# Theta's projection and dense product in scaled fp16 parts, maxima spread through the product banks, and a new order

## Chip, cores and metric

One Trainium2 chip, one of its cores. The metric is the device time of one execution in microseconds, here the median of several. The inputs are drawn anew by a fixed rule and are float32 and float64 on the host's side; the output is float32.

## What is computed

The reference is bucketed attention followed by a mixing block, cut here to its formulas (B=4 batches, H=8 heads, S=768 positions, D=64, model width 512):

```python
mask = q_bucket[:, :, :, None] == k_bucket[:, :, None, :]      # 6 sign bits of q @ proj, k @ proj
scores = np.where(mask, scale * np.matmul(q, k.transpose(0, 1, 3, 2)), -1000000000.0)
attn = np.exp(scores - np.max(scores, axis=-1, keepdims=True))
attn = attn / (np.sum(attn, axis=-1, keepdims=True) + 1e-09)
x = np.matmul(attn, v)                                         # then laid out as B, S, H * D
theta = x @ w_theta
zr, zi = x * np.cos(theta), x * np.sin(theta)
u = x + np.einsum('ts,bsd->btd', w_tok_r, zr) + np.einsum('ts,bsd->btd', w_tok_i, zi)
return (u + np.maximum(u @ w_ch, 0.0)).astype(np.float32)
```

## The kernel before, in words

The work is a list of small operations, each for one engine. A table of numbers, `ORDER`, gives the order in which they are issued; every engine works through its own share of it in that order, and an instruction that waits holds back all that stand behind it on its engine. Entries `f0` to `f3` of the table are fillers: one product of constants (`idle_`) of 512 columns into one of the product banks, whose result nobody reads. Nothing is planned at run time.

Attention runs in 96 steps: batch (4) by head pair (4) by query tile (6), two heads to a step. For each head TensorE makes 128 x 768 scores into a pair of PSUM banks (`scores`, operation `dst` for one head in batch 0, `st` for both heads after it), VectorE takes the row maximum, ScalarE the exponential (`pf`) and its fp16 part (`pp`, L704), GpSimd the remainder (L711), a DMA turns both parts, and TensorE sums them with `v` in 18 short products (`pv`). Batch 0 uses float32 scores plus a product of bit codes; batches 1 to 3 use split operands (`hl`) and a mask.

The mixing block of a batch (`moe`) follows its 24 steps and is woven between the steps of the next batch. Per batch there are six token tiles, and for each: four transposes of x (`transposed`, L815), the upper part by ScalarE (L820) and the remainder by VectorE (L824), then twelve products with `w_theta` in three terms, hi·hi, hi·lo and lo·hi (`project`, recorded at L96 as `wth,h_x` and `wth,l_x`), phase and sine (L856, L859, L881), `f`, `z` (L893 to L904), then 36 products of token mixing (`z,wtk`, fp16), `u` (L933), again transposes and parts, twelve products with `w_ch` (`wch,h_u`, `wch,l_u`), the sum with the positive part (`fin`, L945, VectorE) and the store. `h_x`, `l_x`, `wth`, `h_u`, `l_u` and `wch` are float32 words in the rounded format F32R.

PSUM has eight banks: three pairs for scores (`s`) and the rest for products (`m`, four homes). A scale for `v` (16 times) and for the token weights (6 times) needs a maximum over all partitions. `spread_max` makes it: a transpose to one row, a maximum of that row by VectorE, and a product with ones that puts it on every partition. Row and column stand in spare halves of score banks, listed by hand in `SPREAD`. `pow2_scale` then turns the maximum into a power of two and its inverse with three small VectorE operations on 128 partitions.

```python
            terms = [(a, bb, c) for c in range(NC) for a, bb in (("hi", 0), ("hi", 1), ("lo", 0))]
...
                        mm(res["ps"][:, : cols.stop - cols.start], u[a][:, c], w[bb][:, c, cols], n == 0, n == len(terms) - 1)
```

## Time and profile before

| | before |
|---|---|
| median of 3 runs | 734.14 us (729.14 to 736.46) |
| the profiled execution | 729.0 us, of it 727.2 us span |
| TensorE busy | 714.3 us (98%) |
| VectorE / ScalarE / GpSimd busy | 588.3 / 535.4 / 430.3 us |
| granted TensorE clock | 1.00 over the span |

The span runs from the first to the last instruction; 1.8 us of the execution lie around it. Busy times are unions of an engine's instructions. A product's recorded duration contains the time in which the next one already streams, so what a product costs is read from one start to the next, not from its duration.

### The profile page before, as it was taken

How to read it: one execution, taken by the hardware profiler on the slowest of the kernel's cores; microseconds unless marked ns; L12 is line 12 of the kernel's file. 1: busy time of each engine (PE TensorE's matmuls, PEld its weight loads, DVE VectorE, ACT ScalarE, POOL GpSimd, SP SyncE). 2: the span in 40 equal slices, each digit the busy share in tenths (PEclk: the TensorE clock that was granted, in tenths of full speed). 3: DMA queues.
4: the chain of work that ended last, by engine and by line, in shares of the span. 5: the costliest groups of instructions: out<-in, count | busy, mean ns of one | idle time of the engine just before them, and what ended most of it. 6: DMA issues, size and time to landing. Idle time of an engine off the chain costs nothing.

```text
span 727.2 us, 17462 instructions
## 1 busy us (share of the span) xinstructions
PE 714.3 (98%) x6644; PEld 468.2 (64%) x6644; DVE 588.3 (81%) x1343; ACT 535.4 (74%) x718; POOL 430.3 (59%) x461
## 2 busy tenths in 40 slices
PE   8999999999999999999999999999999999999998
PEld 3455555566756566787856676777656676884456
DVE  5879986889999999989888886989997887747223
ACT  3786887979999778778998775778986776756000
POOL 4576576776557776976666767556666666611000
PEclk9999999999999999999999999999999999999999
DMA  8899999997786999999867998997769989940002
GB/s 338 178 213 224 198 184 215 177 239 169 172 180 143 195 216 190 231 195 209 167 113 150 205 169 170 184 209 119 135 125 169 168 169 170 167 95 16 1 0 87
DMA packets 324044, 120.97 MB, mean 166 GB/s; under 512 B 306316, under 2 KB 313848, under 8 KB 323960
## 3 DMA queue, kind: packets, MB, share of 16 engines
q1 hardware_dynamic: 323960, 119.86, 82.1%
q8 instruction: 52, 0.85, 0.5%
q14 instruction: 32, 0.26, 0.1%
HBM read 32.56 MB, written 6.29 MB: 53 GB/s over the span
## 4 chain that ended last, share of the span: by engine, by line
PE 69%; DVE 11%; DMA 8%; ACT 7%; issue 3%; POOL 1%; SPq 0%; DVEq 0%; ACTq 0%; POOLq 0%
PE ps L96 67%; DMA pt<-pp 6%; DVE pf L678 3%; PE ps L815 2%; ACT pp L704 2%; ACT pf L695 2%; DVE mk L674 1%; POOL pp L711 1%; DVE l_x L824 1%; DMA raw<-in_wt_dram 1%; ACT pf L698 1%; DVE f L893 1%; DVE raw L331 1%; DVE vv L404 1%; ACT n L856 1%
## 5 line engine op out<-in xcount | busy, mean ns | idle before, releaser
L711 POOL TENSOR_TENSOR pp<-pf,pp 128x384 f16<-128x384 f32 x372 | 347.1, 957 | 186.5 <-ACT pp L704 141.5
L96 PE MATMUL ps<-z,wtk 128*128 128x512 f16 x864 | 203.2, 379 | 0.4 <-DVE rows L536 0.4
L695 ACT ACTIVATE pf<-pf,mc 128x768 f32<-128x768 f32 x144 | 133.3, 930 | 53.5 <-DVE mc L681 41.5
L704 ACT ACTIVATE pp<-pf 128x768 f16<-128x768 f32 x192 | 159.7, 838 | 15.4 <-DMA pt<-pp 12.9
L678 DVE CUSTOM_DVE_ANT_1 pf<-ps,mk 128x768 f32<-128x768 f32 x144 | 136.6, 952 | 31.7 <-POOL pp L711 15.1
L96 PEld LDWEIGHTS <-pt 128*128 128x128 f16 x3456 | 120.4, 97 | 27.7 <-issue 6.9
L96 PEld LDWEIGHTS <-wtk 128*128 128x128 f16 x864 | 78.6, 98 | 87.4 <-issue 4.0
L96 PE MATMUL ps<-vv,pt 128*128 128x65 f16 (+1 forms) x3456 | 129.5, 193 | 1.0 <-DVE x L933 0.4
L96 PE MATMUL ps<-hl 64*128 64x512 f32 (+1 forms) x864 | 97.7, 352 | 1.3 <-DVE mc L678 1.3
L96 PEld LDWEIGHTS ps<-hl 64*128 64x128 f32 x864 | 73.2, 184 | 27.8 <-issue 9.4
L674 DVE TENSOR_SCALAR mk<-kb,qc 128x768 bf16<-128x768 bf16 x144 | 85.1, 604 | 0.3
L96 PE MATMUL ps<-nat 64*128 64x512 f32 (+1 forms) x192 | 71.0, 506 | 0.3 <-ACT pf L698 0.2
L96 PE MATMUL ps<-wth,h_x 128*128 128x512 f32 x192 | 65.2, 420 | 0.2 <-DVE l_x L824 0.2
L96 PE MATMUL ps<-wch,h_u 128*128 128x512 f32 (+1 forms) x200 | 64.4, 405 | 0.0
L698 ACT ACTIVATE pf<-ps,mc 128x768 f32<-128x768 f32 x48 | 46.9, 985 | 22.5 <-DVE mc L691 16.0
L96 PE MATMUL ps<-idle 128*128 128x512 f16 x196 | 59.6, 391 | 3.4 <-DVE l_x L824 1.2
L904 POOL TENSOR_TENSOR z<-f,z 128x512 f16<-128x512 f32 x25 | 32.3, 1295 | 47.1 <-ACT z L898 34.7
L685 DVE TENSOR_REDUCE mc<-ps 128x1 f32<-128x768 f32 x48 | 45.1, 948 | 11.6 <-PE ps L96 10.5
L820 ACT ACTIVATE h_u<-ps 128x512 fp32r<-128x512 f32 x24 | 14.2, 591 | 50.0 <-PE ps L815 33.8
L96 PEld LDWEIGHTS ps<-nat 64*128 64x128 f32 x192 | 28.8, 186 | 25.9 <-issue 17.9
L893 DVE SCALAR_TENSOR_TENSOR f<-x,zsc,z 128x512 f32<-128x512 f32 x48 | 37.4, 798 | 4.4 <-ACT z L882 2.7
L96 PEld LDWEIGHTS ps<-wch,h_u 128*128 128x128 f32 x200 | 35.7, 188 | 7.8 <-ACT rows L543 0.3
(125 smaller groups left out, 961.5 us busy)
## 6 DMA issues: line engine op xcount, KB each, us to landing
nat<-in_qk_dram SPq DMA_DIRECT2D x32, 384.0 KB, 3.9
raw<-in_wt_dram SPq DMA_DIRECT2D x12, 768.0 KB, 5.1
vb<-in_v_dram SPq DMA_DIRECT2D x16, 384.0 KB, 4.2
out_dram<-x SPq DMA_DIRECT2D x23, 256.0 KB, 2.8
kb<-rows SPq DMA_DIRECT2D x48, 96.0 KB, 2.6
pt<-pp SPq DMA_TRANSPOSE x192, 4.2
w_th<-in_moe_w_theta_dram SPq DMA_DIRECT2D x4, 512.0 KB, 5.5
w_ch<-in_moe_w_ch_dram SPq DMA_DIRECT2D x8, 256.0 KB, 4.0
```

The costliest lines, as they stand in the source:

```text
L96: PE.matmul(out_, l, r, start=start, stop=stop, skip_group_check=True)
L674: DVE.tensor_scalar(u["mk"][:, :, : S // 3], t["code"][:, j].rearrange("p (a n) -> p a n", a=3), t["qc"][:, i, j : j + 1], -APART, ALU.not ...
L678: DVE.tensor_tensor_reduce(u["pf"].rearrange("p (a n) -> p a n", a=3), st[j].rearrange("p (a n) -> p a n", a=3), u["mk"][:, :, : S // 3], ...
L685: DVE.tensor_reduce(col(0), st[j], AX.X, ALU.max, negate=True)
L695: ACT.activation(u["pf"], u["pf"], AF.Exp, bias=col(2), scale=1.0 / math.sqrt(D))
L698: ACT.activation(u["pf"], st[j], AF.Exp, bias=col(2), scale=col(1))
L704: ACT.activation(u["pp"][:, 0], u["pf"], AF.Copy)
L711: return lambda: eng.tensor_tensor(u["pp"][:, 1, cols], u["pf"][:, cols], u["pp"][:, 0, cols], ALU.subtract)
L815: PE.transpose(u["pt"][:, c], src()[:, c * P : (c + 1) * P], ident)
L820: ACT.activation(u["hi"], u["pt"], AF.Copy)
L893: DVE.scalar_tensor_tensor(u["f"], tl[b][:, tt], zsc[:, b : b + 1], t["zw"][r][:, tt], ALU.mult, ALU.mult)
L904: return lambda: eng.tensor_tensor(t["z"][r, 1][:, tt], u["f"], t["z"][r, 0][:, tt], ALU.subtract)
```

## The change

What it does, by parts:

- `wth`, `wch` and the turned parts of x and u become fp16. So that they fit fp16's range, each operand is scaled by powers of two: `w_theta` and `w_ch` by a maximum over all their values (new `prep_theta` and `prep_ch`, in place of `split_weight`), x by the largest scale of its batch, u per row. The scales enter as column operands of operations that were there (`xh`, `xl`, `turns`, `rest`, the sines), which now multiply and subtract instead of only subtracting.
- The dense product's end becomes two operations: `relu` (scale and positive part, ScalarE or VectorE) into a temporary tile, and `fin` (the sum, VectorE or GpSimd).
- `spread_max` takes two short holds of product banks instead of the hand-listed spare halves, and forms the power of two on the one-partition value before it is spread; the maxima become 24 instead of 22.
- Step 0 loads k before q, makes its sign products in another order, and splits both heads' scores into a first part (`dsa`) that doesn't wait for the signs and a second (`dsb`).
- `ORDER` and the numbers behind it are new throughout. It holds 289 fillers instead of 196. The tile counts of `pp` and the slots of the raw weights change with it.

The diff, cut to its core (the table of the order is left out; the rows below show what it does):

```diff
-    wth = [wp.tile([P, NC, DM], F32R, name=f"wth{i}") for i in range(2)]
+    wth = [wp.tile([P, NC, DM], F16, name=f"wth{i}") for i in range(2)]
...
-    def pow2_scale(amax, inv, s):
-        DVE.tensor_scalar(inv, amax, 1e-30, 2.0**-13, ALU.max, ALU.mult)
-        DVE.tensor_scalar(inv.bitcast(U32), inv.bitcast(U32), MASK, None, ALU.bitwise_and)
-        DVE.tensor_scalar(s.bitcast(U32), inv.bitcast(U32), MASK, None, ALU.bitwise_xor)
-
-    def widened(srcs, n, nm, tag, prio, stage="x", by=1.0):
+    def scale_of(col, inv, s):
+        DVE.tensor_copy(inv, col)
+        DVE.tensor_scalar(s.bitcast(U32), col.bitcast(U32), MASK, None, ALU.bitwise_xor)
...
-    def spread_max(own, one, sr, deps, nm, prio, keep=()):
+    def spread_max(own, one, sr, deps, nm, prio, keep=(), n=1, least=LEAST):
 
         t = {}
-        homes = SPREAD[nm].pop(0)
+        sm_, sm2 = Slot("m"), Slot("m")
+        t["slot"] = sm2
 
         def turn_():
-
-            row, col = ((2 * k + 1) * BANK + BANK // 2 + (P if nm == "w" else 0) for k in homes)
-            t["row"], t["col"] = psum[:1, row : row + P], psum[:, col : col + 1]
+            t["row"] = bank(sm_, [P, P], nm + "row")[:1]
             PE.transpose(t["row"], own(), ident)
 
-        o = op(nm + "tr", prio, on("PE", 110, turn_), deps, [sr, *keep])
-
-        o = op(nm + "one", prio, on("DVE", 200, lambda: DVE.tensor_reduce(one, t["row"], AX.X, ALU.max)), [o], [sr])
-        o = op(nm + "br", prio, on("PE", 91, lambda: mm(t["col"], row1, one.bitcast(BF16)[:, 1:2], True, True)), [o], [sr])
+        o = op(nm + "tr", prio, on("PE", 110, turn_), deps, [sr, sm_, *keep])
+        def pow2():
+            DVE.tensor_reduce(one, t["row"].rearrange("p (n a) -> p n a", n=n), AX.X, ALU.max)
+            DVE.tensor_scalar(one, one, least, 2.0**-13, ALU.max, ALU.mult)
+            DVE.tensor_scalar(one.bitcast(U32), one.bitcast(U32), MASK, None, ALU.bitwise_and)
+
+
+        o = op(nm + "one", prio, on("DVE", 420 + 130 * n, pow2), [o], [sr, sm_])
+        def spread_():
+            t["col"] = bank(sm2, [P, P], nm + "col")[:, :1]
+            mm(t["col"], row1, one.bitcast(BF16).rearrange("p (n two) -> p n two", two=2)[:, :, 1], True, True)
+
+        o = op(nm + "br", prio, on("PE", 75, spread_), [o], [sr, sm2])
         return t, o
...
+    def prep_theta(prio0, step_):
...
+                a = op("wload", prio, on("SP", [(450, 640000)], load), slots=[sl])
+                b_ = op("wlow", prio, on("DVE", 350, low), [a], [sl])
+                e = op("whigh", prio, on("DVE", 615, high), [b_], [sl])
+                d = op("wsign", prio, on("ACT", 540, lambda: ACT.activation(t["sg"], t["sg"], AF.Sign)), [e], [sl])
+                e = op("wabs", prio, on("ACT", 650, lambda: ACT.activation(t["f"], t["f"], AF.Abs, scale=1.0 / TWO_PI, accum_out=tam[:, c : c + 1])), [e], [sl])
+                sums.append(e)
+                parts.append((t, sl, op("wmul", prio, {
+                    "POOL": (1000, lambda: POOL.tensor_tensor(t["f"], t["f"], t["sg"], ALU.mult)),
+                    "DVE": (595, lambda: DVE.tensor_tensor(t["f"], t["f"], t["sg"], ALU.mult)),
+                }, [d, e], [sl])))
+
+            piece()
...
+        o = op("wmax", last, on("DVE", 61, lambda: DVE.tensor_reduce(tsc[:, 0:1], tam, AX.X, ALU.max)), sums)
+        sp_, o = spread_max(lambda: tsc[:, 0:1], wone, sr, [o], "w", last)
+        o = op("wscale", last, on("DVE", 125, lambda: scale_of(sp_["col"], tsc[:, 1:2], tsc[:, 2:3])), [o], [sr, sp_["slot"]])
+        for c, (t, sl, m) in enumerate(parts):
+            i = op("wth", last, on("ACT", 640, lambda t=t, c=c: ACT.activation(wth[0][:, c], t["f"], AF.Copy, scale=tsc[:, 2:3])), [m, o], [sl])
+            wready["th"] += [i, op("wtl", last, on("DVE", 640, lambda t=t, c=c: DVE.scalar_tensor_tensor(wth[1][:, c], t["f"], tsc[:, 2:3], wth[0][:, c], ALU.mult, ALU.subtract)), [i], [sl])]
...
+    def prep_ch(prio0, step_):
...
+        o = op("wmax", last, on("DVE", 61, lambda: DVE.tensor_reduce(chs[:, 0:1], cam, AX.X, ALU.max)), sums)
+        sp_, o = spread_max(lambda: chs[:, 0:1], wone, sr, [o], "w", last)
+        o = op("wscale", last, on("DVE", 125, lambda: scale_of(sp_["col"], chs[:, 1:2], chs[:, 2:3])), [o], [sr, sp_["slot"]])
+        for c in range(NC):
+            i = op("wth", last, on("ACT", 640, lambda c=c: ACT.activation(wch[0][:, c], whole()[:, c], AF.Copy, scale=chs[:, 2:3])), [muls[2 * c], muls[2 * c + 1], o])
+            wready["ch"] += [i, op("wtl", last, on("DVE", 640, lambda c=c: DVE.scalar_tensor_tensor(wch[1][:, c], whole()[:, c], chs[:, 2:3], wch[0][:, c], ALU.mult, ALU.subtract)), [i])]
...
+        if g == 0:
+            hs += [plain(1), plain(0)]
...
+            for i, lo, n_ in ((1, 0, 512), (1, 512, S - 512), (0, 0, 2 * P), (0, 2 * P, S - 2 * P)):
+                placed_signs(lo, n_, i)
...
+        ready = t["ready"] + (t.get("late", []) if i > 1 else [])
+        if g == 0:
+            a = op("dsa", g, on("PE", 1300, lambda: scores([0, 1], 0)), t["ready"][:2], ss + t["slots"])
+            a = [op("dsb", g, on("PE", 340, lambda: scores([0, 1], 1)), [a] + ready, ss + t["slots"])] * 2
+        elif g < SH:
+            a = [op("dst", g + DS * j, on("PE", 1650, lambda j=j: scores([j])), ready, [ss[j]] + t["slots"]) for j in range(2)]
...
+            DVE.tensor_scalar(xi, zi, LEAST * 2.0**-13, None, ALU.max)
+            DVE.tensor_scalar(xs.bitcast(U32), xi.bitcast(U32), MASK, None, ALU.bitwise_xor)
+            DVE.tensor_scalar(xr, xs, tsc[:, 2:3], MAGIC, ALU.mult, ALU.mult)
+            DVE.tensor_scalar(xp, xi, tsc[:, 1:2], -0.25 * TURN, ALU.mult, ALU.mult)
...
+            DVE.tensor_scalar(ui[:, lo:hi], winv[:, lo:hi], 2.0**16, 2.0, ALU.mult, ALU.add)
+            DVE.tensor_scalar(ui[:, lo:hi], ui[:, lo:hi], zinv[:, b : b + 1], LEAST * 2.0**-13, ALU.mult, ALU.max)
+            DVE.tensor_scalar(ui[:, lo:hi].bitcast(U32), ui[:, lo:hi].bitcast(U32), MASK, None, ALU.bitwise_and)
+            DVE.tensor_scalar(us[:, lo:hi].bitcast(U32), ui[:, lo:hi].bitcast(U32), MASK, None, ALU.bitwise_xor)
...
+        rscaled = op("rscale", G + at("Y0", b), on("DVE", 133, lambda: DVE.tensor_scalar(rs, ui, chs[:, 1:2], 0.25, ALU.mult, ALU.mult)), scaled + [chscaled])
...
-            b_ = op("xh", prio, on("ACT", 477, high), [a], [sm_, sxt])
-            c = op("xl", prio, on("DVE", 600, lambda: DVE.tensor_tensor(u["lo"], u["pt"], u["hi"].bitcast(F32), ALU.subtract)), [b_], [sm_, sxt])
+            b_ = op("xh", prio, on("ACT", 570, high), [a], [sm_, sxt])
+            c = op("xl", prio, on("DVE", 660, lambda: DVE.scalar_tensor_tensor(u["lo"], u["pt"], scale, u["hi"], ALU.mult, ALU.subtract)), [b_], [sm_, sxt])
...
-                o = op("proj", prio, on("PE", 10 + 690 * (cols.stop - cols.start) / DM, go), (deps + wdeps) if o is None else [o], [sm_, sxt])
+                o = op("theta" if kind == "p" else "proj", prio, on("PE", 7 + 640 * (cols.stop - cols.start) / DM, go), (deps + wdeps) if o is None else [o], [sm_, sxt])
...
-                    ACT.activation(u["n"], res["ps"], AF.Identity, bias=magic)
+                    ACT.activation(u["n"], res["ps"], AF.Identity, bias=xr)
...
-                    ACT.activation(c_, c_, AF.Sin, bias=hpi, scale=-TURN)
-                    ACT.activation(s_, s_, AF.Sin, scale=-TURN)
+                    ACT.activation(c_, c_, AF.Sin, bias=hpi, scale=xp)
+                    ACT.activation(s_, s_, AF.Sin, scale=xp)
...
-                        def fin():
-                            DVE.scalar_tensor_tensor(tl[b][:, to, cols], r_["ps"][:, :n_], 0.0, tl[b][:, to, cols], ALU.max, ALU.add)
-
-                        c = op("fin", prio + 0.2, on("DVE", 70 + 537 * n_ / DM, fin), [pe], [sr, sx])
+                        s1 = Slot("tmp")
+
+                        def relu(e):
+                            def go():
+                                r_["f"] = tmp(f"r_{b}_{to}_{cols.start}", s1)[:, :n_]
+                                if e == "ACT":
+                                    ACT.activation(r_["f"], r_["ps"][:, :n_], AF.Relu, scale=rs[:, to : to + 1])
+                                else:
+                                    DVE.tensor_scalar(r_["f"], r_["ps"][:, :n_], 0.0, rs[:, to : to + 1], ALU.max, ALU.mult)
+                            return go
+
+                        def fin(eng):
+                            return lambda: eng.tensor_tensor(tl[b][:, to, cols], tl[b][:, to, cols], r_["f"], ALU.add)
+
+                        c = op("relu", prio + 0.2, {"ACT": (150 + 420 * n_ / DM, relu("ACT")), "DVE": (120 + 540 * n_ / DM, relu("DVE"))}, [pe, rscaled], [sr, s1])
+                        c = op("fin", prio + 0.2, {"DVE": (60 + 540 * n_ / DM, fin(DVE)), "POOL": (126 + 1100 * n_ / DM, fin(POOL))}, [c], [s1, sx])
...
-BUFS = {'hl': 2, 'rows': 2, 'mc': 3, 'pf': 3, 'pp': 4, 'pt': 4, 'vb': 1, 'tmp': 3, 'mk': 2}
+BUFS = {'hl': 2, 'rows': 2, 'mc': 3, 'pf': 3, 'pp': 6, 'pt': 4, 'vb': 1, 'tmp': 3, 'mk': 2}
+XT = []
```

The numbers of instructions that change on the engines, counted from both programs: TensorE has the same products apart from 93 more fillers and two more maxima (one transpose and one short product each); the 564 products of 512 columns and 24 of 256 with `wth` and `wch` now have a weight load of their own in the program, where a float32 product carries its load. VectorE gains 72 instructions, most of them on one column, and 48 of its 128x512 subtractions become scaled ones; 8 of 25 `relu` and 7 of 25 `fin` are its own, the other `relu` are ScalarE's and the other `fin` GpSimd's. Fillers that stand ahead of certain places, before and after the change: ahead of the first scores of batch 1: 137 and 177; of batch 2: 191 and 251; of batch 3: 194 and 267; at the last scores of batch 3: 195 and 272; ahead of the last product: 196 and 278; behind it 0 and 11. Nineteen more of the fillers than before (48 against 29) stand right ahead of a float32 group (scores, transposes of a maximum, sign products). In the 48 scores of batch 0, five heads stood alone between other work, eleven times two stood together and seven times three; with the change three heads stand alone, eighteen times two stand together and three times three.

TensorE, where the first scores of batch 1 stand (`hl` scores, `ident,x` the transposes of a token tile, `idle` fillers). Before:

```order
L96 LDWEIGHTS idle
L96 MATMUL ps<-idle 128x512
L96 MATMUL ps<-hl_0_1458 128x512 x6
L96 MATMUL ps<-hl_0_1458 128x256 x6
L96 LDWEIGHTS idle
L96 MATMUL ps<-idle 128x512
L96 MATMUL ps<-wth_96,h_x_0_2080 128x512
L96 MATMUL ps<-wth_97,h_x_0_2080 128x512
L96 MATMUL ps<-wth_96,l_x_0_2081 128x512
L815 MATMUL ps<-ident,x_597 128x128 x4
```

and with the change:

```order
L923 MATMUL ps<-ident,x_610 128x128 x4
L94 MATMUL ps<-hl_0_1588 128x512 x6
L94 MATMUL ps<-hl_0_1588 128x256 x6
L94 LDWEIGHTS idle
L94 MATMUL ps<-idle 128x512
L94 LDWEIGHTS h_x_0_2177
L94 MATMUL ps<-wth_94,h_x_0_2177 128x512
L94 LDWEIGHTS h_x_0_2177
L94 MATMUL ps<-wth_95,h_x_0_2177 128x512
L94 LDWEIGHTS h_x_0_2177
L94 MATMUL ps<-wth_94,h_x_0_2177 128x512
```

Here as many fillers stand beside the scores as before, the transposes have moved ahead of them, and each product with `wth` has an fp16 operand and a load ahead of it instead of a float32 operand.

TensorE, in the first dense products (batch 0, woven into batch 1). Before:

```order
L96 MATMUL ps<-wch_3330,h_u_0_4105 128x512
L96 MATMUL ps<-wch_3331,h_u_0_4105 128x512
L96 MATMUL ps<-wch_3330,l_u_0_4106 128x512
L96 MATMUL ps<-hl_3_3467 128x512 x6
L96 MATMUL ps<-hl_3_3467 128x256 x6
L297 MATMUL ps<-ident,vam_0_4428 1x128
L96 MATMUL ps<-wch_3330,h_u_1_4019 128x512
```

and with the change:

```order
L94 LDWEIGHTS h_u_0_4023
L94 MATMUL ps<-chh,h_u_0_4023 128x512
L94 LDWEIGHTS idle
L94 MATMUL ps<-idle 128x512
L94 LDWEIGHTS idle
L94 MATMUL ps<-idle 128x512
L94 LDWEIGHTS keyst
L94 MATMUL ps<-rows_86,keyst 128x384
L94 LDWEIGHTS h_u_0_4023
L94 MATMUL ps<-chh,h_u_0_4023 128x512
```

Two fillers and the bit codes of a later head pair (`keyst`) now split the products of one token tile, where before the products of a tile ran on to the next scores.

VectorE, the first maximum for `v` (`ones` is the value on one partition, `vinv` and `vsc` the two scales, `mc` the row maxima of the scores). Before:

```order
L301 TENSOR_REDUCE ones<-ps 1x1
L691 TENSOR_SCALAR mc_0_0_182<-mc_0_0_182 128x1
L685 TENSOR_REDUCE mc_0_1_205<-ps 128x1
L219 TENSOR_SCALAR vinv<-ps 128x1
L220 TENSOR_SCALAR vinv<-vinv 128x1
L221 TENSOR_SCALAR vsc<-vinv 128x1
```

and with the change:

```order
L276 TENSOR_REDUCE ones<-ps 1x1
L277 TENSOR_SCALAR ones<-ones 1x1
L278 TENSOR_SCALAR ones<-ones 1x1
L765 TENSOR_REDUCE mc_0_1_217<-ps 128x1 x2
L768 TENSOR_SCALAR mc_0_1_217<-mc_0_1_217 128x1
L771 TENSOR_SCALAR mc_0_1_217<-mc_0_1_217 128x1
L218 COPY vinv<-ps 128x1
L219 TENSOR_SCALAR vsc<-ps 128x1
```

Two of the three operations that stood behind the spreading product now stand ahead of it, on one partition, and a copy takes the third's place.

## Rows read from the trace of the kernel before

**Rows 1.** The page's head and its busy times.
```profile
span 727.2 us, 17462 instructions
...
PE 714.3 (98%) x6644; PEld 468.2 (64%) x6644; DVE 588.3 (81%) x1343; ACT 535.4 (74%) x718; POOL 430.3 (59%) x461
```

**Rows 2.** Stretches: length; busy PE, PEld, DVE, ACT, POOL (instructions); clock; DMA share, GB/s.
```profile
0.00:25.00 25.00, 22.81 (x78) 9.98 (x79) 16.45 (x39) 12.14 (x17) 11.91 (x22) 1.00 0.91 312
25.00:130.00 105.00, 103.55 (x960) 57.94 (x959) 89.23 (x207) 84.33 (x110) 69.03 (x70) 1.00 0.98 198
130.00:205.00 75.00, 72.37 (x670) 47.20 (x666) 68.21 (x154) 69.59 (x97) 50.17 (x50) 1.00 0.89 190
205.00:478.00 273.00, 270.65 (x2813) 186.46 (x2812) 242.23 (x574) 221.00 (x304) 188.19 (x202) 1.00 0.94 182
478.00:700.00 222.00, 220.91 (x2013) 148.87 (x2013) 163.28 (x358) 145.96 (x191) 110.95 (x119) 1.00 0.67 122
700.00:727.20 27.20, 23.97 (x124) 17.72 (x122) 8.87 (x14) 2.39 (x4) 0.00 (x0) 1.00 0.16 58
```

**Rows 3.** Groups by line and shape: count | busy us, mean ns | idle before.
```profile
L96 PE MATMUL ps<-z,wtk 128*128 128x512 f16 x864 | 203.2, 379 | 0.4 <-DVE rows L536 0.4
...
L96 PEld LDWEIGHTS <-wtk 128*128 128x128 f16 x864 | 78.6, 98 | 87.4 <-issue 4.0
...
L96 PEld LDWEIGHTS ps<-wth,h_x 128*128 128x128 f32 x192 | 34.8, 189 | 7.6 <-DVE l_x L824 0.7
```

**Rows 4.** TensorE in order of time: last phase products, first token mixing.
```profile
start us, us, engine line op out<-in xcount [idle before <-releaser]
...
650.33 0.39 PE L96 MATMUL ps<-wth,l_x 128*128 128x512 f32 x1
...
657.39 0.39 PE L96 MATMUL ps<-wth,l_x 128*128 128x512 f32 x1
657.62 4.71 PE L96 MATMUL ps<-z,wtk 128*128 128x512 f16 x21
```

**Rows 5.** TensorE in order of time, batch 0: one and three heads' scores.
```profile
44.56 1.12 PE L96 MATMUL ps<-nat 64*128 64x512 f32 x2
...
46.37 1.04 PE L96 MATMUL ps<-idle 128*128 128x512 f16 x4
47.34 1.12 PE L96 MATMUL ps<-nat 64*128 64x512 f32 x2
...
51.74 0.60 PE L96 MATMUL ps<-idle 128*128 128x512 f16 x2
```

**Rows 6.** The same later: small products, fillers, two heads' scores, batch 1's first.
```profile
106.73 0.38 PE L96 MATMUL ps<-idle 128*128 128x512 f16 x1
107.50 0.16 PE L96 MATMUL ps<-ones,row 1*128 1x1 bf16 x1 [0.39 <-DVE mc L685]
...
107.69 0.71 PE L96 MATMUL ps<-vv,pt 128*128 128x65 f16 x18
...
113.08 0.38 PE L96 MATMUL ps<-idle 128*128 128x512 f16 x1
113.39 1.12 PE L96 MATMUL ps<-nat 64*128 64x512 f32 x2
...
116.17 1.25 PE L96 MATMUL ps<-idle 128*128 128x512 f16 x5
...
153.41 1.32 PE L96 MATMUL ps<-hl 64*128 64x512 f32 x12
```

**Rows 7.** VectorE groups, columns as in rows 3.
```profile
L933 DVE SCALAR_TENSOR_TENSOR x<-ps,swt,x 128x512 f32<-128x512 f32 x24 | 17.5, 741 | 23.1 <-PE ps L96 22.9
...
L824 DVE TENSOR_TENSOR l_u<-ps,h_u 128x512 fp32r<-128x512 f32 x24 | 16.4, 685 | 15.2 <-ACT h_u L820 15.2
...
L220 DVE TENSOR_SCALAR vinv<-vinv 128x1 uint32<-128x1 uint32 x16 | 2.5, 154 | 0.6
...
L945 DVE SCALAR_TENSOR_TENSOR x<-ps,x 128x256 f32<-128x256 f32 x2 | 0.8, 424 | 1.7 <-PE ps L96 1.7
```

More of the change, by code (lines that the diff above doesn't have):

```diff
@@ L431, in whole, with plain @@
                 dma(t["nat"][:, i], qk[b, hp, :, i])
-        if direct:
+        def plain(i):
+            def go():
+                if "nat" not in t:
+                    t["nat"] = ap_.tile([P, 2, S], F32, tag=sh.tag, bufs=1, name=f"nat_{b}_{hp}")
+                dma(t["nat"][:, i], qk[b, hp, :, i])
+            return op("qkload", G + QKL, on("SP", [(440, 462000)], go), slots=[sh])
+        if g == 0:
+            hs += [plain(1), plain(0)]
+        elif direct:
             hs.append(op("qkload", G + QKL, on("SP", [(440, 462000)] * 2, whole), slots=[sh]))
@@ L609, in step, with scores @@
         st = [None, None]
-        def scores(heads):
+        def scores(heads, part=None):
             hl = t.get("hl")
-            for j in heads:
-                st[j] = bank(ss[j], [P, S], f"st{j}_{nm}")
+            if part != 1:
+                for j in heads:
+                    st[j] = bank(ss[j], [P, S], f"st{j}_{nm}")
             terms = ((3, 3), (2, 2)) if b == 0 else ((0, 0), (0, 1), (1, 0)) if zp else ((0, 0), (0, 1), (1, 0), (2, 2))
@@ L617, in scores @@
                 for n, (a, c) in enumerate(terms):
+                    if part not in (None, n):
+                        continue
                     for j in heads:
@@ L776, in moe @@
         t = {}
+        xi, xs, xr, xp = (sb[:, b, i : i + 1] for i in range(4))
         def start():
@@ L963, in lsh_attention_moe_kernel @@
         prep_wtok(to, W0 + WS * to)
-    for c in range(NC):
-        split_weight(w_theta, wth, c, (0, DM), "th", "z0", "x", WTH + WTS * c, 1.0 / TWO_PI)
-        for half in range(2):
-            split_weight(w_ch, wch, c, (half * DM // 2, DM // 2), "ch", "tmp", "tmp", WC + WCS * (c + 0.5 * half))
+    thscaled = prep_theta(WTH, WTS)
+    chscaled = prep_ch(WC, WCS)
     g = 0
@@ L1110 @@
 ZH = 0
-PF = -4.327
-KA = 1.634
-KB = 2.875
-KT = 6.015
-KV = 3.514
-KN = 4.375
-DJ = 0.631
-VM = -6.704
-ZP = [4, 5, 6, 7, 8, 9, 10, 11, 12, 13, 14, 15]
-MK = 2.323
-AB = -9.06
-WTH = 15.121
-WTS = -4.433
-WC = 36.148
-WCS = 2.11
+PF = 2.606
+KA = 10.994
+KB = 2.89
+KT = -0.827
+KV = 3.549
+KN = 4.72
+DJ = 0.779
+VM = -5.863
+ZP = [4, 5, 6, 7, 8, 9, 10, 11, 12, 13, 14, 15]
+MK = 2.073
+AB = -4.147
+WTH = 16.675
+WTS = 0.001
+WC = 38.061
+WCS = -2.605
 P1 = [[0, 999, ['ACT']]]
```

399 lines of the change are left out of this document (227 added, 172 removed), and 25 rows, old and new, of the table ORDER.

## Prediction

> **What bounds the kernel now.** I read the page's busy times first, then the busy times by stretch, then TensorE in order of time. TensorE is busy for 714.3 of 727.2 us, and about 42 us of that are the 196 fillers at 0.217 us each [rows 1, 4]. By stretch one sees where its 12.9 idle us lie: 2.2 in the first 25 us, 3.2 behind the last product, and 7.5 in all the rest, never more than 2.7 in one stretch [rows 2]. VectorE is the next in load: 89.2 of 105.0 us between 25 and 130, 68.2 of 75.0 up to 205, and 163.3 of 222.0 after 478 [rows 2]. So TensorE's queue is full from end to end, partly with products that nobody needs, and a filler costs its time whether or not the wait for which it was put there comes. A change of this kernel is therefore counted as what it adds to and takes from TensorE's queue, and then the waits are asked after.
>
> Recorded durations overlap (0.379 us for a token-mixing product [rows 3]), so I price products from start to start. Twenty-one of them take 4.71 us; without the last one's own duration that is (4.71 - 0.38) / 20 = 0.217 us each [rows 4]. From 650.33 to 657.39 run thirty float32-word products with `wth`: 7.06 / 30 = 0.235 us each [rows 4].
>
> **The change, part by part.**
>
> *Theta's and the dense product in fp16.* 564 products of 512 columns and 24 of 256 count as 576 full ones. They become the kind that token mixing is made of, so 0.235 becomes 0.217: 576 x 0.0187 = 10.8 us off the queue. The weight load falls from 0.189 to 0.098 us [rows 3]. It is hidden behind a long product, but in the program before 24 of the groups stand right behind a weighted sum's short products or behind transposes: at most 24 x 0.091 = 2.2 us. I take it whole; 0 is the other bound. From below the fp16 gain is bounded by 0 (the extra load instructions show in the queue and take it all), from above by 13.0.
>
> *The fillers.* 93 more. Eleven stand behind the last product, where the end of the last tile and its store need 3.2 us anyway [rows 2], and 11 x 0.217 = 2.4 fit. The other 82 stand inside the queue: 82 x 0.217 = 17.7 us (40 before batch 1's first scores, 20 before batch 2's, 13 before batch 3's, 9 after). Ahead of a float32 group the next start comes 0.31 us after a filler's (113.08 to 113.39 [rows 6]), and 19 more of them stand so: 19 x 0.095 = 1.8 us.
>
> *Batch 0's scores.* One head alone took 1.81 us (44.56 to 46.37 [rows 5]), two adjoining 2.78 (113.39 to 116.17 [rows 6]), three 4.40 (47.34 to 51.74 [rows 5]). Before: 5 x 1.81 + 11 x 2.78 + 7 x 4.40 = 70.4; with the change 3 x 1.81 + 18 x 2.78 + 3 x 4.40 = 68.7. That is 1.8 less. Step 0's new split can bring its first maximum forward, and the fillers ahead of it fall from 15 to 11; these are in the count of fillers already, and I give the rest nothing.
>
> *Maxima.* Two more, 0.19 us of TensorE each (107.50 to 107.69 [rows 6]): 0.4. Two more one-column VectorE operations, 0.154 us each [rows 7], now stand between the reduction and the spreading product. Other products are queued between the two, so I take nothing; if TensorE stood still for it all 24 times it would be 24 x 0.31 = 7.4 us, and what stands behind it there are weighted sums and scores.
>
> *The rest is VectorE's, ScalarE's and GpSimd's.* 48 subtractions become scaled ones, 0.741 for 0.685 [rows 7]: 2.7 us. `relu` and `fin` move one pass off VectorE for most tiles, and put 17 passes each on ScalarE and GpSimd, which have 191.8 and 296.9 us free [rows 1]. About 45 new one-column operations are 45 x 0.154 = 7 us of VectorE. Nearly all lies beside TensorE's queue. Without that cover, in the last tile, the half `relu` ahead of the sum is one more pass of 0.42 [rows 7]: 0.4 us on the path.
>
> The exception may be batch 0. Charging every VectorE instruction ahead of the 41st row maximum with its kind's mean duration, the new order has about 15 us more there, an estimate from the two orders. VectorE's idle time from 25 to 130 is 15.8 us [rows 2]. The 40 fillers there lengthen the stretch by 40 x 0.217 - 1.8 = 6.9 us, which makes room for part of it; I take no further loss, and put the rest into a rival.
>
> A page bears on this: the Trainium skill's "Perfetto Trace Analysis", section "Identifying the Most-Contended Engine", says that TensorE's matmul busy share misleads and that its weight-load share should be set against the other engines' occupancy. By that, 64% against 81% [rows 1], VectorE would be the engine to count on, and its 15 us would all be on the time, about 744 on the profiled execution's scale. The trace speaks against it for most of the span, since starts follow one another without a gap [rows 4]; for batch 0 it is the third rival below.
>
> **The sum.** 17.7 + 1.8 - 10.8 - 2.2 - 1.8 + 0.4 + 0.4 = +5.5 us. On the profiled execution (727.2 of span and 1.8 around it, 729.0) that is 734.5. This execution lies at the low end of the runs shown: 729.1, 734.1 and 736.5, mean 733.2. From the mean I get 738.7, and that is my number; it is 0.6% over the median of 734.1.
>
> TensorE's waits are taken as unchanged. If none of the 7.5 us were left the sum would be -2; if the many places where new fillers and new operations meet make them twice as long, +13. That is the forecast's own range, 731 to 746.
>
> **The rivals.**
>
> 1. *The fillers cost nothing* (ends on the other side). They would stand where TensorE waited before, so that 19.5 us of them fall into waits. Then the sum is -14.0, and the time 719. For it: they were put where a plan saw TensorE idle, and a wait shows in the records only in part. The spreading product at 107.50 starts 0.77 us after a filler whose place is 0.22 long, and the profile calls 0.39 of these 0.55 us idle [rows 6]. So perhaps as much again as the 7.5 us is hidden in busy time, 15 in all (an estimate). Against it: gaining over 1% needs 12.8 of these 15 to coincide with new fillers, and 40 of the 82 stand in batch 0, where the stretch from 25 to 130 shows 1.5 us of idle [rows 2].
>
> 2. *fp16 gives nothing*: the separate loads take TensorE's queue as long as before. Then the sum is +18.5, 752. Against it stands the token mixing, which has the same loads and shapes and runs at 0.217 [rows 4].
>
> 3. *VectorE becomes the bound in batch 0.* At the share it reached there (89.2 of 105.0 [rows 2]) 15 us of work need 17.6 us, 10.7 more than the 6.9 counted: +16.2, 749. It decides once VectorE can't go much above 85%. For it: products and maxima wait for each other in this stretch. Against it: from 130 to 205 VectorE ran at 91% [rows 2].
>
> 4. *The short holds of product banks* make TensorE stand at each maximum: +5.5 + 7.4, 746.
>
> **How the numbers follow.** Forecast 0.58, rival 1 0.14, rival 2 0.04, rival 3 0.18, rival 4 0.06. About 1%, 7 us, is what a measurement of this kernel tells from no change. Faster by more: nearly all of rival 1, 0.13. Slower by more: the upper fifth of the forecast's own range, 0.12, with rivals 2 to 4, nearly all of which lie there, 0.25: 0.37. Within 1%: 0.50. The range must leave out no more than 0.2: from 724, which cuts most of rival 1, to 751, which cuts rival 2 and a little of rival 3.
>
> **What would show it.** Start to start, a product with `wth` or `wch` should take 0.217 us in a long run; 0.235 would be rival 2. TensorE's busy time should stay near 720 us in a span near 733. The first scores of batch 1, at 153.4 before [rows 6], should come 5 to 8 us later; 15 or more with VectorE above 90% in the first 150 us would be rival 3. Long waits of the spreading product for `ones` would be rival 4. Rival 1 would show as a span below 720 with TensorE's idle time outside the two ends well under 7.5 us. My number is wrong, above all, if the waits change by more than the fillers and the products do.

## The result and the profile after

The changed kernel takes 734.8 us (median of 20 runs, 733.0 to 737.6), the kernel before, run in turn with it, 730.8 us (median of 20). The ratio is 1.0052, interval 1.0039 to 1.0065: slower by 0.52%, or 4.0 us between the medians. The forecast was 738.7 and +5.5 us; within 1%, as it turned out, had a chance of 0.50. In some executions of the experiments the granted clock fell for a few microseconds; where that decides a number it is said beside it. Ratios below are each to the kernel before in the same series of runs, and a difference in us is the difference of ratios times 730.8.

The profiled execution took 733.0 us. The page's head, its busy times and its first DMA queue (share of the time of 16 DMA engines):

```profile
span 731.1 us, 17711 instructions
...
PE 717.9 (98%) x6741; PEld 426.7 (58%) x6741; DVE 601.1 (82%) x1415; ACT 555.2 (76%) x744; POOL 451.9 (62%) x481
...
q1 hardware_dynamic: 323960, 119.86, 82.3%
```

The same stretches as in [rows 2], columns as there:

```profile
0.00:25.00 25.00, 22.09 (x85) 9.42 (x86) 17.34 (x42) 12.26 (x17) 9.64 (x22) 1.00 0.76 281
25.00:130.00 105.00, 101.70 (x881) 55.11 (x880) 89.05 (x215) 82.98 (x108) 59.80 (x66) 1.00 0.97 196
130.00:205.00 75.00, 73.35 (x749) 44.98 (x749) 67.68 (x166) 67.08 (x90) 51.48 (x51) 1.00 0.97 201
205.00:478.00 273.00, 270.13 (x2789) 169.28 (x2787) 244.12 (x602) 230.05 (x318) 196.67 (x208) 1.00 0.91 174
478.00:700.00 222.00, 221.10 (x2090) 132.44 (x2087) 171.69 (x376) 158.19 (x205) 129.80 (x133) 1.00 0.71 127
700.00:731.10 31.10, 29.55 (x157) 15.45 (x155) 11.22 (x17) 4.60 (x8) 4.48 (x4) 1.00 0.22 85
```

TensorE in order of time: batch 1's first scores, and a long run of theta's products:

```profile
163.06 1.32 PE L94 MATMUL ps<-hl 64*128 64x512 f32 x12
...
655.08 4.70 PE L94 MATMUL ps<-wth,h_x 128*128 128x512 f16 x21
659.61 0.81 PE L94 MATMUL ps<-z,wtk 128*128 128x512 f16 x3
```

Taken alone, these lines look as the sum on record wants them. TensorE's busy time is 717.9 (720 were expected), and 21 products take 659.61 - 655.08 = 4.53 us, 0.216 each, as the token mixing does. But batch 1's first scores come at 163.06 instead of 153.41 [rows 6], 9.7 us later where 5 to 8 were expected, and at the end only 3.9 us of span are left of that. So batch 0 loses about 10 us, and the rest of the kernel gains about 6. Theta's and the dense product are the natural place for a gain, but the experiments show that their 13 us did not come.

### The profile page after: what moved, and what is told of

Its sections match the earlier page's. It is cut to its first block, busy times and chain, and to the rows that moved or that the text cites. A ratio compares the mean times of both kernels' runs of the same rounds, so it can differ in the third digit from the quotient of the medians.

```text
span 731.1 us, 17711 instructions
## 1 busy us (share of the span) xinstructions
PE 717.9 (98%) x6741; PEld 426.7 (58%) x6741; DVE 601.1 (82%) x1415; ACT 555.2 (76%) x744; POOL 451.9 (62%) x481
## 4 chain that ended last, share of the span: by engine, by line
PE 62%; DVE 15%; ACT 12%; issue 4%; DMA 3%; POOL 2%; SPq 0%; DVEq 0%; ACTq 0%; POOLq 0%
PE ps L94 60%; DVE pf L758 2%; PE ps L923 2%; ACT pf L775 2%; ACT pp L784 2%; POOL pp L791 2%; DMA pt<-pp 2%; DVE mc L765 1%; DVE mk L754 1%; DVE f L1000 1%; ACT L988 1%; ACT z L988 1%; DMA rawth<-in_moe_w_theta_dram 1%; ACT z L989 1%; ACT z L1005 1%
## 5 line engine op out<-in xcount | busy, mean ns | idle before, releaser
L791 POOL TENSOR_TENSOR pp<-pf,pp 128x384 f16<-128x384 f32 x375 | 350.8, 959 | 180.6 <-ACT pp L784 120.8
L784 ACT ACTIVATE pp<-pf 128x768 f16<-128x768 f32 x192 | 159.5, 839 | 3.4 <-DMA pt<-pp 0.2
L94 PE MATMUL ps<-hl 64*128 64x512 f32 (+1 forms) x864 | 95.6, 351 | 0.0
L94 PE MATMUL ps<-idle 128*128 128x512 f16 x289 | 87.4, 386 | 5.5 <-DVE idle L78 1.1
L94 PE MATMUL ps<-chh,h_u 128*128 128x512 f16 (+1 forms) x300 | 70.4, 371 | 0.0
L94 PE MATMUL ps<-wth,h_x 128*128 128x512 f16 x288 | 69.9, 379 | 0.0
L1011 POOL TENSOR_TENSOR z<-f,z 128x512 f16<-128x512 f32 x28 | 34.5, 1238 | 50.0 <-DVE z L1007 29.3
L927 ACT ACTIVATE h_u<-ps,ust 128x512 f16<-128x512 f32 x24 | 16.3, 677 | 44.1 <-PE ps L923 37.4
L1063 POOL TENSOR_TENSOR x<-x,r 128x512 f32<-128x512 f32 (+1 forms) x18 | 23.3, 1301 | 42.7 <-ACT r L1057 33.7
L94 PEld LDWEIGHTS <-idle 128*128 128x128 f16 x289 | 25.5, 98 | 31.4 <-issue 12.0
L94 PEld LDWEIGHTS <-h_u 128*128 128x128 f16 x300 | 27.8, 98 | 26.7 <-issue 0.6
```

Of the source, the lines that this page charges most:

```text
L94: PE.matmul(out_, l, r, start=start, stop=stop, skip_group_check=True)
L784: ACT.activation(u["pp"][:, 0], u["pf"], AF.Copy)
L791: return lambda: eng.tensor_tensor(u["pp"][:, 1, cols], u["pf"][:, cols], u["pp"][:, 0, cols], ALU.subtract)
L927: ACT.activation(u["hi"], u["pt"], AF.Copy, scale=scale)
L1011: return lambda: eng.tensor_tensor(t["z"][r, 1][:, tt], u["f"], t["z"][r, 0][:, tt], ALU.subtract)
L1063: return lambda: eng.tensor_tensor(tl[b][:, to, cols], tl[b][:, to, cols], r_["f"], ALU.add)
```

## The experiments

Fillers are taken out of `ORDER` or put in; "batch 1" below is the start of batch 1's first scores in the profiled execution, 153.4 in the kernel before and 163.1 in the changed one. It scatters: e1, e7 and e12 change nothing ahead of it, and it comes 0.8 to 0.9 us later in them (163.9, 154.2 and 154.3), so a difference of less than about 1 us says nothing.

### Fillers behind batch 1's first scores

e1 takes all 101 out of the changed kernel up to the last product, e4 all 59 out of the kernel before. Part of a row of the table, in e1:

```diff
-784 f2 828:0 2593:2 2584:0 765:0 837:1 827:0.1 783 94 2585 791:0 98 f1 1098:0
+784 828:0 2593:2 2584:0 765:0 837:1 827:0.1 783 94 2585 791:0 98 1098:0
```

> The changed kernel without the 101 fillers between the first scores of batch 1 and the last product; the 177 ahead of them and the 11 behind the last product stay. Full-queue theory (each filler costs its 0.217 us): 101 x 0.217 = 21.9 us less than the changed kernel, about 713. Rival (they stand where TensorE waits anyway): within 2 us of the changed kernel, about 734, with TensorE's idle time up by some 20 us.

> The kernel before without its 59 fillers behind the first scores of batch 1. Full-queue theory: 59 x 0.217 = 12.8 us less, about 718. Rival (they stand in waits): within 2 us of the kernel before, about 730.

e1: 732.9 us, ratio 1.0023 (1.0007 to 1.0038); against 1.0052 that is 2.1 us for 101 fillers, 0.02 us each instead of 0.217. e4: 729.8 us, 0.9976 (0.9956 to 0.9996), 1.8 us for 59. In e1 the clock was full in nine of ten executions, in e4 in none (0.986 to 0.998), so e4's gain may be too small by what the clock took. TensorE's busy time in e1 by stretch, and what it now waits for (us in total, times, longest):

```profile
205.00:478.00 273.00, 260.60 (x2718) 163.67 (x2716) 244.90 (x603) 230.29 (x319) 196.57 (x208) 1.00 0.91 174
478.00:700.00 222.00, 219.33 (x2079) 131.53 (x2076) 171.39 (x378) 158.06 (x205) 129.56 (x133) 1.00 0.69 127
```
```profile
PE ps L94 <- DMA pt<-pp: 4.8, 7, 1.2
PE ps L94 <- DVE mc L758: 3.0, 5, 1.0
PE ps L94 <- DVE z L966: 2.7, 4, 1.2
```

Between 205 and 478 TensorE is busy for 260.6 us instead of 270.1, and the stretch is done no sooner (VectorE has the same work in it, 244.9 and 244.1 us): the fillers had mostly stood where TensorE waits for turned parts, row maxima and phases. Their length was hidden in busy time, and a busy share of 98% said nothing of it.

### fp16 products alone

e3 gives the kernel before fp16 operands without scales, in the old order; e8 takes e4's fillers away too; e19 is e8 again, beside e18.

```diff
-    wth = [wp.tile([P, NC, DM], F32R, name=f"wth{i}") for i in range(2)]
+    wth = [wp.tile([P, NC, DM], F16, name=f"wth{i}") for i in range(2)]
...
-                u["hi"] = mp.tile([P, NC, P], F32R, tag="h" + sxt.tag, name=f"h_{nm}")
+                u["hi"] = mp.tile([P, NC, P], F16, tag="h" + sxt.tag, name=f"h_{nm}")
```

> The kernel before in its own order, with only the operands of theta's projection and of the dense product made fp16 (no scales, so small remainders lose digits; no other part of the change). Full-queue theory: 10.8 us from the pace of the products and up to 2.2 from the loads, 11 to 13 us less, about 718 to 720. Rival (the separate weight loads take it back): no change. A third outcome, half of it or less, would mean that TensorE then waits for the other engines.

> The kernel before with fp16 operands for theta's projection and the dense product (no scales) and without its 59 fillers behind batch 1's first scores: e3 and e4 together. Alone these gave -3.5 and -1.8 us. If they are separate gains: -5 to -6 us. If both only free the same slack of TensorE: -3 to -4 us. If TensorE, emptier by 26 us, falls to the lower clock in places: more than the kernel before with e3 alone, -2 to +3 us. TensorE's full queue would say -24 us.

> The kernel of e8 again, beside e18 on the same chip: 725 to 727 us, and a clock a little below 1.00.

e3: 728.1 us, 0.9953 (0.9936 to 0.9970), 3.4 us and not 13. The stretch from 478 to 700 in e3, and what TensorE waits for over the whole span:

```profile
478.00:700.00 222.00, 217.74 (x2015) 129.71 (x2013) 163.72 (x362) 146.54 (x192) 110.62 (x119) 1.00 0.68 122
```
```profile
PE ps L96 <- DMA pt<-pp: 3.3, 4, 1.4
PE ps L96 <- DVE l_x L824: 2.5, 3, 1.1
PE ps L96 <- DVE mc L678: 2.1, 4, 1.0
```

The same three waits in the kernel before:

```profile
PE ps L96 <- DVE l_x L824: 1.4, 3, 0.7
PE ps L96 <- DVE mc L678: 1.3, 4, 0.5
...
PE ps L96 <- DMA pt<-pp: 0.3, 1, 0.3
```

From 478 to 700 TensorE is busy for 3.2 us less than in [rows 2], and VectorE does the same work there: the products are faster, and TensorE waits longer for what it waited for before. A part of the missing gain is the clock. Seven of e3's ten executions ran at 0.997 to 0.999, the profiled one at 0.68 from 135 to 140, and its batch 1 starts at 155.4, 2.0 us later than before. The three at 1.00 took 725.3 to 727.4 us, and the kernel before at 1.00 in the same series 730.8 (median): about 4.5 us at a full clock (an estimate from three executions), still a third of 13. e8: 725.9 us, 0.9925 (0.9901 to 0.9950); e19: 725.5, 0.9921 (0.9892 to 0.9951), both at 0.988 to 0.998 in all executions. Taking some 24 us of TensorE's queue away gives 5.5 to 5.8 us, about the two parts added (3.4 and 1.8). e8 is faster than both kernels, and it is the old order with fewer products.

### Fillers in batch 0

e2 takes every second one out of the changed kernel's batch 0 (78), e13 only 40 between steps 9 and 20; e16 doubles 40 in the kernel before, the number by which the change exceeds it there. A part of a row in e16:

```diff
-431 440 42 f2 424G 441 397:0 f2 453:0 442:0 f2 369 425D f2 443:0 f2 50 f2 426:1 f2 432 f2 163
+431 440 42 f2 424G 441 397:0 f2 453:0 442:0 f2 f2 369 425D f2 443:0 f2 f2 50 f2 426:1 f2 f2 432 f2 163
```

> The changed kernel without every second filler from the 21st to the 177th (78 of them, all ahead of batch 1's first scores). Full-queue theory: 78 x 0.217 = 16.9 us less, about 718. Rival (batch 0 is paced by the other engines and its fillers lie in TensorE's waits): within 2 us, about 734, and batch 1's first scores stay at 163.

> The changed kernel without every second filler between steps 9 and 20 of batch 0 (40 fillers, 8.7 us of TensorE's queue). TensorE's queue paces there: batch 1's first scores 8 us earlier, whole -6 to -8. Several engines equally close: -2 to -4 at batch 1's first scores (in e2 the same stretch, steps 9 to 18, became 3.2 us shorter with 28 fillers less), whole -1 to -4. The order's waits alone: 0. If the granted clock falls the run is +2 or worse.

> The kernel before with 40 more fillers in batch 0 (steps 8 to 24, each doubling one that is there; 8.7 us of TensorE's queue), the number that the change adds there. TensorE's full queue, as in the sum on record: batch 1's first scores +8.7 us, whole +8 to +9. Fillers fall into waits: 0 to +2. Several engines equally close: +3 to +6, half of their length.

e16: 737.8 us, 1.0102 (1.0068 to 1.0137), 7.5 us for 40 fillers or 0.19 each; batch 1's scores follow at 159.5:

```profile
159.46 1.31 PE L96 MATMUL ps<-hl 64*128 64x512 f32 x12
```

So a filler added in batch 0 costs nearly its length, as the sum had it; behind batch 0 fillers were only taken away (e1, e4), none added. Taking them away in batch 0 does not give it back. e2 took 737.5 us, 1.0076 (1.0045 to 1.0107). Its stretches:

```profile
60.00:130.00 70.00, 64.34 (x624) 36.55 (x623) 61.78 (x149) 55.55 (x70) 44.49 (x46) 1.00 0.97 192
130.00:135.00 5.00, 5.00 (x19) 2.29 (x17) 4.46 (x10) 2.55 (x5) 2.31 (x3) 0.58 1.20 245
135.00:140.00 5.00, 3.81 (x41) 2.50 (x38) 2.02 (x10) 2.72 (x5) 1.71 (x3) 0.74 0.61 116
```

The clock had fallen three times ahead of 60 (to 0.52 from 35 to 40). From 60 to 130 it is full, and from the first row maximum of step 9 to that of step 18 it takes 57.0 us instead of the changed kernel's 60.4: 3.4 us for 31 fillers less, half of their 6.7 us. Then TensorE stands still for 1.58 us:

```profile
129.34 1.12 PE L94 MATMUL ps<-nat 64*128 64x512 f32 x2 [1.58 <-ACT pf L778]
```

and the granted clock is 0.58 and 0.74 in the next two stretches, which means that it ran at the lower level (1.2 GHz) for most of them. The Trainium skill's "TensorE: Matmul & The Clock Gate", section "HAM oscillation — how this bites in real kernels", says that a wait for data between bursts of products can bring TensorE's clock down; this trace has a fall right behind such a wait, though a shorter one than in the page's example, and that the wait is its cause is not shown (e18 and the last section). e13 shows both sides in one kernel: 736.1 us, 1.0062 (1.0031 to 1.0093), but the four executions whose clock stayed at 1.00 took 731.1 to 733.5, the five with 0.988 to 0.995 took 735.7 to 739.2, and one with 0.982 took 743.4. At 1.00 it lies 2.3 us over the kernel before (medians 732.3 and 730.0 in its series), where the changed kernel lies 4.0 over it. Its profiled one (clock 1.00) has batch 1's first scores at 160.5, 2.5 us earlier for 8.7 us of fillers. Fillers added in batch 0 are paid for with most of their length, and taken away they give little back. They also go with the clock: it was below 1.00 in two of twenty executions of the changed kernel (0.998), in all eight of e2 and in six of ten of e13.

e18 puts four fillers ahead of the place where e8 had stood still. In e8's profile:

```profile
130.00:132.00 2.00, 2.00 (x17) 1.06 (x13) 1.96 (x6) 1.00 (x2) 0.45 (x1) 1.00 1.29 225
132.00:134.00 2.00, 1.06 (x4) 0.39 (x3) 1.56 (x4) 2.00 (x5) 1.73 (x2) 0.94 0.94 249
134.00:140.00 6.00, 6.00 (x46) 3.63 (x45) 3.77 (x6) 4.46 (x7) 4.31 (x5) 0.50 0.68 134
```
```diff
-687 695:2 f2 611 712:1
+687 695:2 f2 f2 f2 f2 f2 611 712:1
```

> The kernel of e8 (before with fp16 products and without the late fillers, 725.9 us) with four more fillers at 128.8 us, ahead of the place where TensorE stood still for 0.94 of 2 us (132 to 134) and the granted clock was 0.50 from 134 to 140 in e8's profile. If the stop brings the clock down: no fall there, clock nearer to 1.00 over the run, 723 to 725 us, and batch 1's first scores 1 to 3 us earlier than in e8 (157.0). If the clock falls for other reasons: as e8, or 0.9 us longer for the four fillers.

725.2 us, 0.9915 (0.9892 to 0.9938), and e19 beside it 725.5. Neither profile has the fall at 134, and both have shorter ones later (0.66 from 210 to 215, in e19 also from 170 to 175), so e18 doesn't show what brings a fall. But e19 is e8's program without that fall, and its batch 1 starts at 154.2 instead of 157.0: 2.8 us for some 6 us at the lower clock.

### VectorE's load in batch 0

The stretch up to batch 1's first scores, of the kernel before and then of the changed one, columns as in [rows 2]:

```profile
0.00:153.40 153.40, 148.61 (x1245) 80.34 (x1245) 125.63 (x293) 116.94 (x152) 98.49 (x108) 1.00 0.97 214
```
```profile
0.00:163.10 163.10, 155.80 (x1294) 83.87 (x1294) 135.13 (x335) 120.95 (x160) 92.75 (x110) 1.00 0.93 209
```

VectorE is busy for 9.5 us more in a stretch that is 9.7 us longer, with the same idle time (27.8 and 28.0): this pointed to rival 3. e5 adds ten passes of 0.95 us to the kernel before in batch 0, e7 the same in steps 74 to 92, e6 takes work from the changed kernel.

```diff
                 def shift():
                     DVE.tensor_scalar(col(2), col(0), SHIFT, col(1), ALU.add, ALU.mult)
+                    if j == 0 and 10 <= g < 20:
+                        DVE.tensor_reduce(more_, ident.unsqueeze(1).to_broadcast([P, 6, P]), AX.X, ALU.max)
```
```diff
-                    DVE.scalar_tensor_tensor(t["lo"], t["hi"], 3, t["lo"], ALU.logical_shift_left, ALU.bitwise_xor)
+                    n = 1 if 2 * to + r < 9 else S
+                    DVE.scalar_tensor_tensor(t["lo"][:, :n], t["hi"][:, :n], 3, t["lo"][:, :n], ALU.logical_shift_left, ALU.bitwise_xor)
```

> The kernel before with ten more VectorE passes of about 0.95 us (a maximum over 768 constant columns), one in each of the steps 10 to 19 of batch 0, behind the first head's shift. That is the 9.5 us by which VectorE is busier in the changed kernel ahead of batch 1's first scores (135.1 against 125.6 us, idle 28.0 against 27.8). VectorE paces batch 0 (rival 3): batch 1's first scores come 8 to 10 us later than in the kernel before, and the whole takes +4 to +10 us. TensorE's full queue (the theory on record): the passes fall into VectorE's 28 idle us, batch 1's first scores and the whole move by less than 1.5 us.

> The changed kernel with about 11.5 us less of VectorE in batch 0: the shift that joins the words of the token weights is done for one column only in the first nine pieces (9 x 0.88 us), and so is the remainder of theta's fp16 parts (4 x 0.95 us), which GpSimd sets to zero at the start; so the token mixing and theta's low part are computed with other numbers. VectorE paces batch 0: batch 1's first scores come 8 to 11 us earlier than in the changed kernel (153 to 155 instead of 163), the whole -3 to -9 us. TensorE's full queue: within 1.5 us of the changed kernel.

> The kernel before with the same ten VectorE passes (9.5 us), now one in every second step from 74 to 92, where VectorE is busy for 163 of 222 us. If VectorE paces only where it is most loaded: +0 to +2 us. If each step's chain through the row maximum paces everywhere, so that what delays it is paid: +5 to +10 us. TensorE's full queue: 0 to +1.5 us.

e6: 732.8 us, 1.0014 (0.9992 to 1.0036), 2.8 us less than the changed kernel. VectorE's stretch and batch 1's first scores in e6:

```profile
25.00:130.00 105.00, 101.92 (x901) 56.05 (x901) 81.05 (x213) 82.33 (x108) 59.61 (x66) 1.00 0.97 195
```
```profile
161.92 1.31 PE L94 MATMUL ps<-hl 64*128 64x512 f32 x12
```

VectorE has 8 us less to do there (89.05 in the changed kernel), 10.8 less up to batch 1's first scores (124.4 and 135.1), and these come 1.1 us earlier, hardly more than the scatter. Rival 3 in its plain form falls. e5: 734.3 us, 1.0042 (1.0015 to 1.0070), but its three executions with a full clock took 730.7 to 733.3, at most 2.1 us over the kernel before (731.1 in that series), and its profiled one (clock 0.83 from 80 to 130) lost 10.5 us. e7: 734.3 us, 1.0053 (1.0031 to 1.0074), 3.9 us for 9.5, where VectorE is idle for a quarter of the time. Part of that is the clock again: with 1.00 the executions took 732.2 to 734.8, 1.1 to 3.7 us over the kernel before. Some of a pass is paid even there.

### The DMA engines' load

The transfers that turn `pp` into `pt` and the loads fill, in the changed kernel, 0.97 of the DMA engines' time from 25 to 205 and 0.91 from there to 478; in the kernel before it is 0.89 to 0.98 [rows 2], not the 94 to 100% of e9's expectation. e9 and e10 halve eight turning transfers in batch 0 of the kernel before and of the changed one, e12 eight late ones, e11 adds eight loads to e3.

```diff
+                    if j == 1 and 12 <= g < 20:
+                        dma(u["pt"][:, :T], u["pp"][:, 0], transpose=True)
+                        return
                     dma(u["pt"], u["pp"].rearrange("p a s -> p (a s)"), transpose=True)
```
```diff
                     dma(u["pt"], u["pp"].rearrange("p a s -> p (a s)"), transpose=True)
+                    if j == 0 and 12 <= g < 20:
+                        dma(more_.rearrange("p h t d -> p h (t d)"), v[b, 2 * hp : 2 * hp + 2].rearrange("h (p t) d -> p h (t d)", t=T))
```

> The kernel before, in which the second head's transfer that turns pp into pt moves only the upper half in the steps 12 to 19 (eight transfers of 1.17 us of the DMA engines instead of 2.34), and the weighted sum uses that half twice there; so in these steps the lower parts are left out of the result. The transfers pace batch 0 (the DMA engines are 94 to 100% busy up to 478 us): batch 1's first scores come 6 to 9.5 us earlier, the whole -5 to -9.5. TensorE's or VectorE's load paces it: within 1.5 us of the kernel before.

> The same eight half transfers in the changed kernel (9.4 us less of the DMA engines in the steps 12 to 19; lower parts left out there). The transfers pace batch 0, where the change put 12.3 MB into the steps 12 to 19 in place of 8.8: batch 1's first scores come 6 to 9.5 us earlier than in the changed kernel (154 to 157 instead of 163), the whole -4 to -9. Loads of other engines, or the order itself, pace it: within 1.5 us of the changed kernel.

> The kernel of e3 (before with fp16 products, 728.1 us there) with eight more loads of 384 KB in the steps 12 to 19, one behind the first head's turning transfer, into a tile that nobody reads: about 1.4 us of the DMA engines each by the loads of v and of q and k, 11 in all. The transfers pace batch 0: batch 1's first scores 8 to 11 us later than in e3, the whole +6 to +11. Otherwise: within 1.5 us of e3.

> The kernel before with the half transfers of e9 in the second head of the steps 76, 78 to 90, where the DMA engines are busy for 0.67 of the time (again 9.4 us less of them; lower parts left out there). If transfers pace only where their engines are full: 0 to -2 us. If it is the way of each step through its transfer (its duration, not the load) that paces: -4 to -9 us.

e9: 729.7 us, 0.9978 (0.9966 to 0.9990), and batch 1's scores at 153.9, no earlier. e10: 734.3, 1.0036 (1.0017 to 1.0055), which doesn't exclude the changed kernel's 1.0052, and the scores at 163.9, no earlier either. e12: 729.4, 0.9979 (0.9963 to 0.9996). So 9.4 us less gives 1.2 to 1.6 us, wherever. e11: 735.2, 1.0049 (1.0030 to 1.0069); against e3's 0.9953 that is 7.0 us for 11, and batch 1's scores come 5.9 us later than in e3. A part of it is the clock, 0.991 to 0.998 in all nine executions: in e11's profile it is 0.77 and 0.55 from 135 to 145, in e3's 0.98 and 0.68 from 130 to 140, some 3.4 us more at half the clock, so at most 1.7 of the 5.9 (an estimate from these rows). The Trainium skill's "Perfetto Trace Analysis", section "Identifying the Most-Contended Engine", warns that the occupancy of sixteen DMA engines misleads; e9, e10 and e12 agree for what is taken away, and e11 shows that added transfers are paid for all the same.

### Both loads of batch 0 together

e17 is the kernel before with e16's fillers and e5's passes, e14 the changed kernel without e13's fillers and without e6's work.

> The changed kernel with e13's 40 fillers and e6's VectorE work (about 10.6 us in batch 0) both left out; e6 alone gave -2, and its first scores of batch 1 came 1.2 us earlier. Several engines equally close: clearly more than both apart, batch 1's first scores 6 to 10 us earlier than in the changed kernel, whole -4 to -8. The order's own waits: no more than the sum of both apart (-3 to -5 at batch 1, whole -3 to -5). TensorE's queue alone: as e13.

> The kernel before with e16's 40 fillers and e5's ten VectorE passes (9.5 us) in batch 0 together: the loads that the change adds to batch 0, in the old order. e5 alone gave +1.5 where the clock stayed. If these loads are the cause of the 9.7 us at batch 1's first scores: +7 to +11 there, whole +4 to +9. If the new order itself is: no more than e16 and e5 together, +2 to +5.

e17: 738.5 us, 1.0105 (1.0077 to 1.0133), and batch 1's first scores at 162.2, 8.8 us later than before; the change has 9.7. So the old order with the loads that the change adds to batch 0 loses there about what the change loses. Of it e16 alone has 6.1; VectorE's passes add 2.7, and with 40 fillers in place the clock stays at 0.998 or more. e14: 738.5 us, 1.0102 (1.0050 to 1.0153); the clock fell in every execution (0.984 to 0.993), so it leaves open what both removals would give at a full clock.

## Why the prediction was right or wrong

**The premise.** "So TensorE's queue is full from end to end" was read from busy time, and it is the step that failed. Where a product stands ready but its operands come late, busy time does not tell; e1, e3, e4 and e8 take 11 to 24 us from that queue and get back 2 to 6; e1 alone, at a full clock, gets 2.1 for 21.9. The sign that was at hand is on record in favour of rival 1: 0.77 us from a filler to the next product, 0.39 of it idle [rows 6]. The prediction took it as a single case; behind batch 0 most of the fillers' length turned out to stand in waits.

**The fillers, 17.7 + 1.8.** Right in size for the 40 of batch 0: 8.7 forecast, 7.5 measured in the old order (e16). Wrong for the 42 later ones: 9.1 forecast, and at the rate of e1 0.9 (an estimate, 42 of 101 times 2.1, and by removal: no run added a filler there). The 1.8 for fillers ahead of float32 groups was not tried alone. This is rival 1's mechanism, in three batches of four, and what was put against it (that 40 stand where there is no idle time) was right for the fourth.

**fp16, -10.8 and the loads, -2.2.** The pitch is right (0.216), the gain is 3.4 us instead of 13.0 (e3), some 4.5 at a full clock: the products ended sooner and TensorE waited.

**Batch 0's VectorE, taken at nothing beyond the cover.** The estimate of 15 us more was 9.5. It costs 2.7 us at batch 1's first scores on top of the fillers (e17 against e16), and at the end the two cannot be told apart (1.0105 and 1.0102). The rival's price of 10.7 was too high, since most of the work has cover; so was the other reading on record, 15 us of VectorE all on the time.

**The maxima.** Taken at 0.4 with no standing still, rival 4 at 7.4. In the waits of TensorE over the whole span of the changed kernel, the longest single wait and the lines that belong to maxima (L272 is the transpose of one, L276 reads the row, L219 the spread column) are:

```profile
PE ps L94 <- DVE kb L570: 1.3, 1, 1.3
...
PE ps L272 <- DVE x L845: 0.5, 1, 0.5
...
PE ps L272 <- DVE wmx L379: 0.5, 1, 0.5
...
PE ps L94 <- DVE ones L276: 0.4, 1, 0.4
PE ps L94 <- DVE tsc L219: 0.4, 1, 0.4
PE ps L94 <- DVE vsc L219: 0.3, 1, 0.3
PE ps L94 <- DVE wsc L219: 0.3, 1, 0.3
```

For maxima six single waits, 2.4 us in all, where the kernel before has one of 0.39 [rows 6]. The last four, 1.4 us, are fillers that stand until the row or column in a held bank is read, which is what rival 4 describes, at 4 of 24 maxima. So rival 4 came in a small part, about 2 us of standing still against its 7.4. No run undid the holds, so this rests on the waits alone, and what they cost in time is not shown.

**The sum.** +5.5 was forecast, +4.0 measured, and this nearness is no merit: some 11 us of fillers that are not paid (19.5 forecast, 7.5 and 0.9 by the runs) and 9.6 us of fp16 that are not gained nearly cancel. From the runs the account is +7.7 (e17), -3.4 (e3), +0.9 (late fillers): +5.2, or +4.1 with e3 at a full clock, where the ratio of 1.0052 is +3.8. The difference of 0.3 to 1.4 is less than e17's interval allows (2 us to either side), so nothing is left that must be put down to the rest of the change (new order, batch 0's scores, step 0, maxima, `relu` and `fin`). That was not tried alone, and whether the parts add in the new order as in the old was not tested either.

**The base.** 733.2, the mean of the three runs shown, lies 2.4 us above the median of twenty; of the 3.9 us by which 738.7 missed, 2.4 are that and 1.5 the sum.

**What stays open.** Why 9 to 11 us taken from VectorE, from the transfers or from the fillers of the changed kernel's batch 0 bring batch 1's first scores forward by at most 2.5 us each, while the same put into the old order sets them back by 2.7 to 6.1. In batch 0 all but e9's transfers was added to the old order and taken from the new one, so whether it is adding against removing, or the one order against the other, is not separated. It fits several engines standing close behind one another, so that each takes over when another is relieved; e14, which should have shown it, lost its clock.
